# A list scheduler's positions, rounded to six decimals, in a fused attention and gated feed-forward kernel

## The chip, the cores and the metric

The kernel runs on one core of one Trainium2 chip. The metric is the device time of one execution in microseconds, the median of several runs. The profile is one more execution, taken by the hardware profiler; its durations are those of that execution.

## The reference, cut to what matters

Eight batches of eight heads, 1024 positions, head size 64. Keys and values are first projected along the sequence to 64 rows (E and F), then comes attention over those 64, and its output goes through a gated feed-forward layer.

```python
k_proj = einsum('ks,bhsd->bhkd', E, k)
v_proj = einsum('ks,bhsd->bhkd', F, v)
scores = (q @ k_proj.T) / sqrt(64)                  # per batch and head: 1024 x 64
attn = exp(scores - max) ; attn = attn / (sum + 1e-9)
x = attn @ v_proj                                   # -> 8192 tokens x 512
gate = 1 / (1 + exp(-(x @ w_gate)))                 # 512 -> 1536
out = (gate * (x @ w_val)) @ w_out                  # 1536 -> 512, float32
```

## The kernel before, in words

Each batch's 1024 tokens make two blocks of 512, so there are 16 blocks. The feed-forward layer is done block by block, mostly as Strassen-Winograd products with seven multiplications in place of eight: `quad_jobs(K)` makes a third of a block's hidden layer (three K to a block), with one call of `seven` for the gate (W = "G") and one for the value ("V"). The seven products are called A11, A12, S2, S1, S3, A22 and S4 after their left factor. They run on TensorE (PE) into PSUM banks; ScalarE (ACT) copies and snapshots the banks and takes the tanh; VectorE (DVE) adds partial results (`plus`, line 1156) and multiplies value by gate into `hT` (line 1225). `o_jobs(blk)` makes the output product of a block in the same way (sums of `hT` in `s_sum`, line 557, on VectorE or GpSimd (POOL); merges on VectorE, line 1414), or as a plain product (`o_plain`); SyncE (SP) issues the stores.

The attention of a batch is made while the feed-forward layer of the batch before is running. `kv_jobs` or `apart_jobs` project keys and values (`kpd`, `vpD`). `score_jobs` makes eight score tiles: `score` on PE (`kpD`, `qT`), then on VectorE the row maximum (`highest`, line 1645) and its subtraction in the bank (`lower`, line 1672), then the exponential on ScalarE into `pt` (which shares the memory `KVs`), and a DMA transpose to `eT`. `out_jobs` makes twelve out tiles: `outs` on PE (`vpD`, `eT`), reciprocals of the sums on VectorE (`invert`, line 1717), the division on VectorE or, after a copy by ScalarE, on GpSimd (`divide`, line 1734), and a DMA transpose to `xT`, from which the next batch's blocks read. All matmuls have line 528, all ScalarE operations line 542, GpSimd's loads line 569: they are issued by helpers.

None of this code fixes the order of the instructions. Each piece is a `Job` with an engine, a position `pos` on a common axis (one unit is about a sixth of a batch; the positions are sums of tuned offsets from the tables `AT` and `FB`) and the order of its creation, `rank`. `Scheduler.run` walks through a planned time: for each free engine it takes the first job, by position and then by rank, whose inputs are planned to be ready, whose PSUM bank or buffer is free, and whose position is not above that of the first matmul job not yet placed by more than `window` (43.429). The instructions are then issued in the order of the planned starts, and each engine runs its own in that order, waiting on semaphores. So one engine's order also decides which bank or buffer a job gets, when it comes free, and what can be taken next.

```python
for item in sorted(self.open[e], key=lambda i: (i[0], i[1])):   # position, then rank
    if item[0] > limit and not self.running(item[3]):
        continue
    if item[2] <= t + 1e-9 and self.take(item[3], t):
        best = item
        break
```

The positions are binary floating-point sums such as `pos + step * i + lag`, taken in different orders in different places.

Of the kernel before, what the change touches and what calls it, by code (L numbers as in the profile page):

```python
# [54 lines left out]
class Plan:  # L55
# [3 lines left out]
    def __init__(self):  # L59
        self.ops = []  # L60
        self.writers = {}
        self.readers = {}
        self.dma_count = {}
# [89 lines left out]

class Job:
    def __init__(self, eng, pos, body, release, name):
        self.eng, self.pos, self.body, self.release, self.name = eng, pos, body, release, name
        self.cost, self.bytes, self.dma, self.port = 0.0, 0, False, False
        self.deps, self.slots, self.start, self.end = {}, [], None, None

# [1755 lines left out]
```

## Time and profile before

| what | value |
|---|---|
| median of 3 runs | 528.46 us (528.36 to 530.05) |
| the profiled execution | 528.95 us |
| its span, first to last instruction | 527.2 us |
| mean granted TensorE clock | 0.997 |
| TensorE matmuls | 513.4 us busy, 4784 |
| VectorE | 448.3 us busy, 845 |
| ScalarE | 374.6 us busy, 716 and one table load |
| GpSimd | 166.0 us busy, 194 |

How to read it: busy times are sums over the span; matmuls overlap (one of 256 columns is listed with 273 ns, though the next starts earlier), so that their rate is read from start to start. In the views of waits, "A <- B: total, times, longest" says how long engine A stood still until B released it. In a timeline, "x12" are equal instructions that follow each other, and brackets hold the idle time ahead of the first and what ended it. The chain of waits is followed back from the last instruction. "xT", "hT", "KVs" and so on are the names of tiles; pF and pA are the two sets of four PSUM banks.

### The profile page before, as it was taken

The numbers are of one execution on the slowest core, as the hardware profiler recorded it, in microseconds if no ns is written. First come the engines' busy times: TensorE is split into PE (matmuls) and PEld (weight loads), VectorE is DVE, ScalarE is ACT, GpSimd is POOL, SyncE is SP. The second block draws the span as 40 slices with busy tenths as digits, with TensorE's granted clock in tenths as the row PEclk, the third lists the DMA queues.
The fourth block names the chain that finished last, engine by engine and source line by source line (L and its number), as shares of the span: only waits on it lengthen the run. The fifth ranks groups of instructions, "written<-read, shape, count | busy, mean of one in ns | idle before, by whom it ended". The sixth has DMA issues, their size and how long they took to land.

```text
span 527.2 us, 12327 instructions
## 1 busy us (share of the span) xinstructions
PE 513.4 (97%) x4784; PEld 427.8 (81%) x4784; DVE 448.3 (85%) x845; ACT 374.6 (71%) x717; POOL 166.0 (31%) x194
## 2 busy tenths in 40 slices
PE   5999999999979999999999999999999999999998
PEld 4655876888758888888898888888888888888885
DVE  5889997696898879997999879988799969998770
ACT  1565866688747789676976779766896679776852
POOL 9841006602156023540246003460235302530110
PEclk9999999999989999999999999999999999999999
DMA  9999917795478936899269973799177992711104
GB/s 164 197 199 207 194 35 163 165 203 99 71 170 134 202 86 102 171 188 194 49 116 174 185 149 62 181 161 234 33 116 164 182 195 49 141 54 41 41 2 160
DMA packets 140523, 71.59 MB, mean 136 GB/s; under 512 B 97200, under 2 KB 132272, under 8 KB 140464
## 3 DMA queue, kind: packets, MB, share of 16 engines
q0 software_dynamic: 35904, 29.89, 37.4%
q1 hardware_dynamic: 104560, 40.91, 36.7%
q8 instruction: 38, 0.62, 0.5%
q14 instruction: 21, 0.17, 0.1%
HBM read 60.29 MB, written 16.78 MB: 146 GB/s over the span
## 4 chain that ended last, share of the span: by engine, by line
PE 94%; DVE 4%; DMA 1%; ACT 0%; issue 0%; SPq 0%
PE pA L528 50%; PE pF L528 44%; DVE hT L1225 1%; DVE hS L557 1%; DMA EF<-in_F_dram 1%; DVE topf L1645 1%; DVE pA L1672 0%; DVE spare L1156 0%; DVE KVs L1734 0%; DVE ost L1414 0%; DVE pF L1672 0%; DVE inv L1717 0%; ACT ost L542 0%; DVE xS L557 0%; DVE pA L1156 0%
## 5 line engine op out<-in xcount | busy, mean ns | idle before, releaser
L557 POOL TENSOR_TENSOR hT<-hT,hS 128x512 bf16<-128x512 bf16 x42 | 50.3, 1219 | 224.9 <-PE pA L528 127.5
L542 ACT ACTIVATE spare<-pF 128x512 f32<-128x512 f32 (+2 forms) x164 | 91.5, 576 | 22.0 <-PE pF L528 14.9
L542 ACT ACTIVATE spare<-pA 128x512 f32<-128x512 f32 (+2 forms) x151 | 85.9, 581 | 25.7 <-PE pA L528 18.9
L542 ACT ACTIVATE spare<-spare 128x512 f32<-128x512 f32 x76 | 48.2, 634 | 17.3 <-DVE spare L1156 16.9
L528 PE MATMUL pA<-wO,hT 128*128 128x256 bf16 (+1 forms) x396 | 57.2, 289 | 0.2 <-ACT ost L542 0.2
L1734 POOL TENSOR_TENSOR KVs<-spare,inv 128x256 bf16<-128x256 f32 (+1 forms) x47 | 33.5, 720 | 64.2 <-ACT spare L542 39.3
L1156 DVE TENSOR_TENSOR spare<-pF,spare 128x512 f32<-128x512 f32 x60 | 40.8, 683 | 11.0 <-ACT spare L542 3.8
L1156 DVE TENSOR_TENSOR spare<-pA,spare 128x512 f32<-128x512 f32 x55 | 37.4, 682 | 11.9 <-ACT spare L542 4.5
L528 PEld LDWEIGHTS pA<-wO,hT 128*128 128x128 bf16 x396 | 38.1, 98 | 10.4 <-ACT ost L542 0.4
L1225 DVE SCALAR_TENSOR_TENSOR hT<-spare,pF 128x512 bf16<-128x512 f32 x59 | 39.7, 679 | 2.2 <-PE pF L528 0.6
L1225 DVE SCALAR_TENSOR_TENSOR hT<-spare,pA 128x512 bf16<-128x512 f32 x55 | 37.1, 680 | 4.9 <-PE pA L528 2.2
L528 PE MATMUL pF<-xT,wG 128*128 128x256 bf16 (+1 forms) x212 | 35.4, 289 | 0.0
L528 PE MATMUL pF<-xT,wV 128*128 128x256 bf16 (+1 forms) x208 | 34.6, 287 | 0.0
L528 PE MATMUL pF<-wO,hT 128*128 128x256 bf16 (+1 forms) x216 | 31.4, 291 | 0.9 <-DVE hT L1225 0.9
L528 PE MATMUL pA<-xT,wV 128*128 128x256 bf16 (+1 forms) x200 | 32.2, 284 | 0.0
L528 PE MATMUL pA<-xT,wG 128*128 128x256 bf16 (+1 forms) x196 | 31.3, 282 | 0.0
L528 PE MATMUL pF<-xS,wV 128*128 128x256 bf16 x200 | 29.9, 273 | 0.0
L528 PE MATMUL pA<-wT,hS 128*128 128x256 bf16 x216 | 29.2, 273 | 0.3 <-DVE hS L557 0.3
L528 PE MATMUL pF<-xS,tG 128*128 128x256 bf16 x192 | 28.8, 273 | 0.0
L528 PE MATMUL pA<-xS,tV 128*128 128x256 bf16 x184 | 27.6, 273 | 0.0
L528 PE MATMUL pF<-xS,wG 128*128 128x256 bf16 x184 | 27.3, 273 | 0.1
L528 PE MATMUL pA<-xS,wG 128*128 128x256 bf16 x176 | 26.3, 273 | 0.1
(177 smaller groups left out, 1295.6 us busy)
## 6 DMA issues: line engine op xcount, KB each, us to landing
out_dram<-ost SPq DMA_DIRECT2D x63, 256.0 KB, 2.4
KVs<-in_v_dram POOLq DMA_DIRECT2D x15, 512.0 KB, 9.4
KVs<-in_k_dram POOLq DMA_DIRECT2D x14, 512.0 KB, 6.9
Qb<-in_q_dram POOLq DMA_DIRECT2D x14, 512.0 KB, 12.8
wO<-in_moe_w_out_dram POOLq DMA_DIRECT2D x1, 1536.0 KB, 28.6
wG<-in_moe_w_gate_dram POOLq DMA_DIRECT2D x5, 256.0 KB, 16.6
wV<-in_moe_w_val_dram POOLq DMA_DIRECT2D x5, 256.0 KB, 17.2
KVs<-in_k_dram POOLq DMA_DIRECT2D x4, 256.0 KB, 6.6
```

What stands on the lines that cost most here:

```text
L528: lambda e: e.matmul(o, lhsT, rhs, **kw),
L542: lambda e: e.activation(o, i, func, scale=scale),
L557: fn = lambda e: e.tensor_tensor(o, a, b, op)
L1156: lambda e: e.tensor_tensor(PB(b)[:, :] if stay else BF(s), PB(b)[:, :], BF(s), ALU.add),
L1225: lambda e: e.scalar_tensor_tensor(o, y.rearrange("p (j c) -> p j c", j=2), 1.0, x.rearrange("p (j c) -> p j c", j=2), ALU.add, ALU.mult,),
L1645: lambda e: e.tensor_reduce((top if by_pe(b, t, y) else topf)[:, n : n + 8], PB(bk)[:, :].rearrange("p (n k) -> p n k", n=8), mybir.AxisLi ...
L1734: fn = lambda e: e.tensor_tensor(xto.rearrange("p (g h d) -> p h g d", g=2, h=H)[:, hh[0] : hh[1], :, :], o[:, :, 0:DH].rearrange("p (h g) ...
```

## The change

`Job` rounds its position to six decimals when it is made. Nothing else is touched.

```diff
 class Job:
     def __init__(self, eng, pos, body, release, name):
-        self.eng, self.pos, self.body, self.release, self.name = eng, pos, body, release, name
+        self.eng, self.pos, self.body, self.release, self.name = eng, round(pos, 6), body, release, name
         self.cost, self.bytes, self.dma, self.port = 0.0, 0, False, False
```

The offsets in the tables have three decimals, so many positions are equal as decimal numbers though their sums differ in the last bit: there are 212 groups of such positions on one engine. Before, the last bit decides which job of a group comes first; now they are equal and the order of creation decides. In 34 of the 212 groups this turns the order round: 25 on TensorE, 6 on VectorE, 3 on ScalarE. The first in time is a pair of value products of two neighbouring thirds of a block, `VA22` of K = 2 at 5.619 and `VS3` of K = 1 at 5.619000000000001; others come back in each batch, such as `GS2` and `GA12` at 16.969, 22.969 and 28.969. No operation, shape, engine or DMA is added or removed. Since `run` places each job with what is free at that moment, the order after a turned pair can differ from there on.

## The prediction

> **What bounds the kernel now.** I read the page first, then the busy times by stretch, then the waits and the chain of the one stretch that differs from its neighbours, then the order of the instructions in the two built programs.
>
> The page's first lines:
>
> ```profile
> span 527.2 us, 12327 instructions
> PE 513.4 (97%) x4784; PEld 427.8 (81%) x4784; DVE 448.3 (85%) x845; ACT 374.6 (71%) x717; POOL 166.0 (31%) x194
> ```
>
> TensorE is the bound as a whole. A reordering adds and removes no instruction, so it can only change the time in which TensorE stands still. Busy times by stretch of one batch, with the mean granted clock after POOL, show where that is:
>
> ```profile
> core 0: us, PE busy (x) PEld busy (x) DVE busy (x) ACT busy (x) POOL busy (x), PEclk, DMA share, GB/s
> 126.00:187.10 61.10, 56.90 (x519) 47.42 (x518) 53.01 (x95) 41.88 (x81) 19.82 (x22) 0.97 0.73 137
> 187.10:248.10 61.00, 61.00 (x587) 53.39 (x586) 54.74 (x102) 46.80 (x91) 19.83 (x22) 1.00 0.81 146
> ...
> ```
>
> The later batches are full: 61.00 of 61.00 us, 587 matmuls. The stretch from 126 to 187 is not: 56.90 of 61.10, 519 matmuls, and a clock of 0.97. What a better order can win lies there (and a little near 85 us); what a worse order can lose lies anywhere. TensorE's waits in that stretch:
>
> ```profile
> PE pF L528 <- ACT spare L542: 1.1, 3, 0.6
> PE pF L528 <- DVE hT L1225: 0.9, 1, 0.9
> PE pF L528 <- DVE inv L1717: 0.6, 1, 0.6
> PE pA L528 <- ACT ost L542: 0.6, 1, 0.6
> PE pA L528 <- ACT spare L542: 0.5, 1, 0.5
> ```
>
> Many short waits for different things mean that one engine behind them is full. The chain of waits of this stretch names it: from 133.91 to 154.02 nearly every piece is VectorE's.
>
> ```profile
> 133.91 0.70 DVE topf L1645
> ...
> 152.56 0.61 DVE pA L1156
> 153.17 0.10 DVE inv L1717
> 153.27 0.70 DVE hT L1225
> 153.97 0.04 issue
> 154.02 3.69 PE pF L528 x20
> ```
>
> And the windows of these two pieces:
>
> ```profile
> 133.71:154.02 20.31, 16.20 (x158) 12.70 (x155) 20.07 (x45) 12.53 (x25) 5.33 (x8) 0.98 0.65 128
> 154.02:157.00 2.98, 2.98 (x16) 2.16 (x17) 2.98 (x5) 0.55 (x1) 1.88 (x2) 0.54 0.98 188
> ```
>
> VectorE works 20.07 of 20.31 us; then TensorE runs 3 us at 0.54 of its clock. Why the work piles up there is in VectorE's timeline just before: it waits for score tiles of batch 2 that come one by one.
>
> ```profile
> 127.57 0.69 DVE L1645 TENSOR_REDUCE topf<-pA 128x8 f32<-128x512 f32 x1 [2.01 <-PE pA L528]
> ...
> 131.07 0.69 DVE L1645 TENSOR_REDUCE topf<-pA 128x8 f32<-128x512 f32 x1 [1.60 <-PE pA L528]
> ...
> 133.91 0.69 DVE L1645 TENSOR_REDUCE topf<-pA 128x8 f32<-128x512 f32 x1 [1.42 <-PE pA L528]
> ```
>
> That is 5.03 us of idle time on the engine that is then 20 us behind.
>
> **The change, step by step.** It removes and adds nothing: both programs have 4784 matmuls, 845 VectorE and 716 ScalarE operations and the same DMAs. It decides ties. The first matmul that moves is the 541st, at 64.29 us. Leaving bank and buffer names aside, 651 of 4784 matmuls stand elsewhere, 575 of them before the 1651st (192.50 us); from there on 76 of 3134 move, 20 of 535 VectorE operations and 12 of 481 on ScalarE. GpSimd's and SyncE's queues differ only up to their 84th and 45th instruction.
>
> Term A, the pile at 134 us. In the order of before, the eight score tiles of batch 2 begin at matmuls 1094, 1128, 1156, 1170, 1178, 1188, 1192, 1196 (counted from 0), and the first outs follow at 1212: five tiles bunched, 12 matmuls ahead of the work that follows them. In the changed order they begin at 1072, 1088, 1100, 1114, 1130, 1142, 1146, 1156, and the first outs come at 1200, 40 matmuls behind the last. Price of before: from matmul 1160 (133.71) to 1313 there are 102 of 256 columns, 20 of 128 and 32 of 130. TensorE's timeline gives 0.109 us for the first kind (12 from 143.74 to 145.05), 0.055 for the second (4 from 136.34 to 136.56), 0.06 for the third (3 from 147.67 to 147.85): 11.12 + 1.10 + 1.92 = 14.1 us. They took 20.31, so 6.2 us are lost. In the changed order VectorE has 51 operations from the first tile's maximum to the last hT that the O product of block 3 needs: 34 on 512 fp32 at 0.60 (start to start: 137.04, 137.64, 138.24), 12 reciprocals at 0.10, 4 divides at 0.46, one short sum at 0.34: 23.8 us. TensorE has 266 matmuls beside them: 206 × 0.109 + 28 × 0.055 + 32 × 0.06 = 25.9 us. VectorE has 2.1 us to spare where it was 6 short; in the tightest piece (24 operations, 12.8 us, beside 148 matmuls, 13.9) it has 1.1. Term A is -6.2; if the spare time is used up by queueing, -4.8.
>
> Term B, the slow clock. Matmuls 1314 to 1333 took 3.69 us (chain above) and are worth 20 × 0.109 = 2.18: 1.5 us. It came right after 4 us in which PE was busy for 1.98. Without the pile I take it as gone: -1.5, or 0 if it has another cause. [...]
>
> Term C, two gaps near 85 us.
>
> ```profile
> 83.25 2.77 PE L528 MATMUL pA<-wO,hT 128*128 128x512 bf16 x12 [0.22 <-ACT ost L542]
> ...
> 91.56 1.48 PE L528 MATMUL pF<-wT,hT 128*128 128x256 bf16 x12 [0.69 <-ACT spare L542]
> ```
>
> The first waits for its bank, which the plain O product just before used; in the changed order that product takes another bank: 0.22 gone. The second waits for the snapshot of the bank that it goes on in; 8 matmuls of 130 columns now stand between, 8 × 0.06 = 0.48 of cover: 0.2 stays. Term C is -0.7.
>
> Term D, what gets tighter. The second attention transpose (xT) of batch 1 is issued at 89.43, lands a median 3.3 us later (3.0 to 4.6 in the trace) and is used at 94.66: 1.9 us to spare. In the changed order 52 matmuls instead of 76 lie between its last outs and that use, 4.9 us instead of 7.5. The path there is a reciprocal (0.19), a copy (0.39), a divide on GpSimd (0.61), its queueing, and 3.3 of landing: 4.8 to 5.3 us. I take +0.3; bounds 0 and +1.6 (a landing of 4.6). A merge of an O bank just ahead has about 2 matmuls too little cover: +0.2. Small waits in the new order of 64 to 190 us: +0.2, from 0 to 1.
>
> Term E, the repeating batches: the same sequence but for the 76 swapped matmuls, whose TensorE waits in before are at most the 0.25 at 285.53. 0, within ±0.5.
>
> Sum: -6.2 - 1.5 - 0.7 + 0.3 + 0.2 + 0.2 = -7.7. The profiled execution took 528.95 us (span 527.2 and 1.75 around it): 521.3 by its measure. It lies 0.49 above the median of 528.46, so the forecast of a median is 520.8.
>
> **The rivals.** Part is given back: the xT transpose lands late (+1.3 over what I took), and VectorE loses time beside GpSimd. The timeline has one such case: a short hS sum of 0.41 us takes 2.87 at 282.86 while GpSimd runs two hT sums of 2.29 together. In the changed order three of GpSimd's hT sums stand in a row in the O product of block 1, beside VectorE's own; one collision costs 2.87 - 0.41 = 2.5. Time: 522.1 with the first, 524.6 with both. Against it: only one of the two lies where cover is thin. [...]
>
> The slow clock stays though the pile goes: 520.8 + 1.5 = 522.3. [...] Against it: it is the only slow stretch inside the trace, and it starts in the worst 4 us of TensorE.
>
> The pile only moves. VectorE's 448.3 us are the same, and if its 51 operations take 8% longer than the 23.8 us, they exceed TensorE's 25.9 and the jam forms a few us later: 527 to 530. Against it: VectorE's idle 5.03 us before the pile are now used.
>
> Slower: the swapped matmuls of the repeating part hold back a late score tile in each of the five later batches, as batch 2 had it. Price: 7.7 each, 5 × 7.7 = 38.5, so 520.8 + 38.5 = 559. It decides once the stall passes 1.5 us in a batch, which eats the gain. Against it: VectorE is busy 54.74 of 61.00 us there, and the score tiles and outs of the later batches stand at the same places in both orders.
>
> That the change does nothing is out: the two orders differ.
>
> **How the numbers follow.** Forecast as summed 0.69, part given back 0.14, slow clock stays 0.05, pile moves 0.05, slower 0.07. This kernel can be told from no change from about 0.3% on, 1.6 us: faster means under 526.9. The first three are faster, 0.88; a moved pile is the same, 0.05; the last is 0.07. The low end is 520.8 less the 0.7 of term D, if none of it comes true, the 0.5 of term E, and the 0.1 by which the fastest run of before lies under its median: 519.5. The high end takes in both give-backs (524.6) and the 0.5 of term E: 525.1. Left out are the last two rivals and the tails.
>
> **What would show it.** Right: the stretch of batch 2 full like its neighbours (over 580 matmuls in 61 us), no slow clock inside, VectorE off the chain, one gap of about 0.2 near 91 us, the later batches unchanged. Wrong: a DMA wait on xT near 93 us (term D), a clock under 1 with no pile (term B), VectorE on the chain around 130 us (term A), or PE below 61.0 in any later batch (term E).

## The result, and the profile after

The changed kernel takes 520.15 us (median of 4 runs, 519.96 to 520.69) beside 529.25 us for the kernel before on the same chip: a ratio of 0.983, 95% interval 0.9807 to 0.9853. (The 529.25 is the median of four runs; the 528.46 of the table above was that of the first three, with the same spread, 528.36 to 530.05.) The forecast was 520.8. The profiled execution of after took 519.99 us, span 518.2.

The page of after, span and busy times, and the engines' shares of the chain that ended last:

```profile
span 518.2 us, 12331 instructions
PE 509.5 (98%) x4784; PEld 427.8 (83%) x4784; DVE 446.7 (86%) x845; ACT 373.9 (72%) x717; POOL 164.5 (32%) x194
...
PE 98%; DMA 1%; ACT 0%; SPq 0%; issue 0%
```

The work is the same, and VectorE (4% of the chain before) has gone from the chain. The busy times by stretch, of after, in the columns of before:

```profile
126.00:187.10 61.10, 61.10 (x592) 53.73 (x590) 55.90 (x104) 46.58 (x90) 19.94 (x23) 1.00 0.73 143
187.10:248.10 61.00, 61.00 (x588) 53.54 (x586) 54.97 (x103) 46.78 (x91) 20.02 (x23) 1.00 0.75 143
```

The stretch of batch 2 had 56.90 us of TensorE, 519 matmuls and a clock of 0.97. It is now as full as its neighbour: 592 matmuls, clock 1.00. TensorE's waits in the whole of after:

```profile
PE pF L528 <- DMA EF<-in_F_dram: 5.7, 1, 5.7
PE pF L528 <- ACT EF L542: 0.2, 1, 0.2
```

Only the first load and the 0.22 us near 91 us that the prediction left standing remain.

Where the 9 us went is read from the start of the n-th matmul in both traces, after less before: +0.21 at the 60th (the first load), -0.67 at the 800th, -8.38 at the 1440th, -8.97 at the last. So terms C and D give -0.88, A and B -7.71, the later batches -0.59. Inside A and B, the 1314th to 1334th matmul took 3.52 us before and 2.22 after: the clock is 1.3 of it, the stall 6.4.

TensorE's timeline shows what the order did at that place. Before, from 147.67 us on (start, duration, tile, brackets: idle time ahead and what ended it):

```profile
147.67 0.34 PE L528 MATMUL pF<-vpD,eT 128*128 128x130 bf16 x3
...
148.28 0.34 PE L528 MATMUL pF<-vpD,eT 128*128 128x130 bf16 x3
149.17 0.29 PE L528 MATMUL pF<-vpD,eT 128*128 128x130 bf16 x2 [0.56 <-ACT spare L542]
150.10 0.34 PE L528 MATMUL pF<-vpD,eT 128*128 128x130 bf16 x3 [0.64 <-DVE inv L1717]
150.60 0.34 PE L528 MATMUL pF<-vpD,eT 128*128 128x130 bf16 x3 [0.16 <-ACT spare L542]
150.78 0.28 PE L528 MATMUL pA<-vpD,eT 128*128 128x130 bf16 x2
151.40 0.34 PE L528 MATMUL pF<-vpD,eT 128*128 128x130 bf16 x3 [0.34 <-ACT spare L542]
152.28 0.34 PE L528 MATMUL pA<-vpD,eT 128*128 128x130 bf16 x3 [0.55 <-ACT spare L542]
152.62 0.29 PE L528 MATMUL pF<-vpD,eT 128*128 128x130 bf16 x2
152.75 0.38 PE L528 MATMUL pF<-wO,hT 128*128 128x256 bf16 x2
154.02 2.32 PE L528 MATMUL pF<-wO,hT 128*128 128x256 bf16 x10 [0.89 <-DVE hT L1225]
```

These are out tiles (`outs`), from 148.28 on eight of them directly behind one another on three banks (pF2, pF3 and pA3). Each tile's matmuls are worth 0.12 to 0.17 us, and five of the eight tiles stand still until a bank has been through a reciprocal on VectorE and a copy or a division. The same tiles in after, to the start of the second gap between them:

```profile
136.28 0.34 PE L528 MATMUL pF<-vpD,eT 128*128 128x130 bf16 x3
136.45 0.45 PE L528 MATMUL pA<-vpD,eT 128*128 128x130 bf16 x5
136.84 0.83 PE L528 MATMUL pA<-wT,hT 128*128 128x256 bf16 x6
137.51 0.60 PE L528 MATMUL pA<-xS,wG 128*128 128x256 bf16 x4
137.95 0.34 PE L528 MATMUL pF<-vpD,eT 128*128 128x130 bf16 x3
138.12 0.46 PE L528 MATMUL pA<-vpD,eT 128*128 128x130 bf16 x5
138.42 0.60 PE L528 MATMUL pF<-xS,tV 128*128 128x256 bf16 x4
```

At most three stand in a row, and 6 to 16 matmuls of products come before the next ones. No bracket is left.

What did not change is how long a bank is held. One tile divided by VectorE, its reciprocal and its division, in before and then in after:

```profile
148.74 0.18 DVE L1717 RECIPROCAL inv<-pF 128x6 f32<-128x6 f32 x1
149.41 0.55 DVE L1734 TENSOR_TENSOR KVs<-pF,inv 128x384 bf16<-128x384 f32 x1
```

```profile
136.83 0.30 DVE L1717 RECIPROCAL inv<-pA 128x6 f32<-128x6 f32 x2
137.62 0.55 DVE L1734 TENSOR_TENSOR KVs<-pA,inv 128x384 bf16<-128x384 f32 x1
```

From the start of the tile's last matmul (148.40 and 136.57) to the end of the division, this turn took 1.56 us before and 1.60 after. Counted to the end of the last operation that reads the bank, the nine tiles of before from 147.67 on took 1.04 to 2.02 us, median 1.33, and the twelve of after 1.06 to 1.97, median 1.31. So no engine serves a bank faster in the new order: TensorE has other matmuls to run during the turn.

### The profile page after: what moved, and what is told of

The parts are those of the page before. It is cut to its first block, busy times and chain, and to the rows that moved or that the text cites. A ratio compares the mean times of both kernels' runs of the same rounds, so it can differ in the third digit from the quotient of the medians.

```text
span 518.2 us, 12331 instructions
## 1 busy us (share of the span) xinstructions
PE 509.5 (98%) x4784; PEld 427.8 (83%) x4784; DVE 446.7 (86%) x845; ACT 373.9 (72%) x717; POOL 164.5 (32%) x194
## 4 chain that ended last, share of the span: by engine, by line
PE 98%; DMA 1%; ACT 0%; SPq 0%; issue 0%
PE pF L528 50%; PE pA L528 48%; DMA EF<-in_F_dram 1%; ACT EF L542 0%; SPq L629 0%; ACT ost L542 0%
## 5 line engine op out<-in xcount | busy, mean ns | idle before, releaser
L542 ACT ACTIVATE spare<-pF 128x512 f32<-128x512 f32 (+2 forms) x179 | 101.0, 582 | 27.0 <-PE pF L528 18.1
L542 ACT ACTIVATE spare<-pA 128x512 f32<-128x512 f32 (+2 forms) x139 | 79.0, 577 | 24.5 <-PE pA L528 16.5
L1156 DVE TENSOR_TENSOR spare<-pA,spare 128x512 f32<-128x512 f32 x72 | 48.7, 681 | 13.5 <-PE pA L528 6.5
L1734 POOL TENSOR_TENSOR KVs<-spare,inv 128x384 bf16<-128x384 f32 (+1 forms) x50 | 36.3, 732 | 67.7 <-ACT spare L542 46.2
L528 PE MATMUL pA<-wO,hT 128*128 128x256 bf16 (+1 forms) x348 | 49.3, 287 | 0.0
L528 PE MATMUL pA<-xS,wG 128*128 128x256 bf16 x264 | 39.2, 273 | 0.0
L1156 DVE TENSOR_TENSOR spare<-pF,spare 128x512 f32<-128x512 f32 x41 | 28.0, 683 | 7.9 <-ACT spare L542 5.2
L528 PE MATMUL pF<-xS,tV 128*128 128x256 bf16 x224 | 33.6, 273 | 0.0
L528 PEld LDWEIGHTS pF<-wO,hT 128*128 128x128 bf16 x264 | 25.4, 98 | 6.4
L528 PEld LDWEIGHTS pA<-xS,wG 128*128 128x128 bf16 x264 | 25.2, 98 | 5.1 <-issue 2.3
```

The lines of the kernel that those rows point to most:

```text
L528: lambda e: e.matmul(o, lhsT, rhs, **kw),
L542: lambda e: e.activation(o, i, func, scale=scale),
L1156: lambda e: e.tensor_tensor(PB(b)[:, :] if stay else BF(s), PB(b)[:, :], BF(s), ALU.add),
L1734: fn = lambda e: e.tensor_tensor(xto.rearrange("p (g h d) -> p h g d", g=2, h=H)[:, hh[0] : hh[1], :, :], o[:, :, 0:DH].rearrange("p (h g) ...
```

## The experiments

**One pair or many?** Of the 34 turned groups the first (the pair VA22 and VS3 at 5.619) was turned alone in e1, and all but it in e2.

```diff
 # e1
+        pos = round(pos, 6) if 5.6185 < pos < 5.6195 else pos
 # e2
+        pos = pos if 5.6185 < pos < 5.6195 else round(pos, 6)
```

> Of the 34 turned groups only the first pair (VA22 and VS3 at 5.619) is turned; all other positions keep their last bits. Planned order: 150 TensorE jobs stand elsewhere than before, 22 elsewhere than in the changed kernel (late ones); GpSimd's and SyncE's orders equal those of the changed kernel. Theory (this pair sets the order of the bank grants up to batch 2, and so takes away the pile of VectorE work): 520 to 521.2 us, the stretch of batch 2 full at 61 us of TensorE, no slow clock in it; the late 22 jobs are worth at most the 0.6 us by which the later batches ran ahead. Rival (several turned pairs are needed): between 524 and 529 us, with part of the pile left.

> All positions are rounded but those of that pair. Planned order: 24 TensorE jobs stand elsewhere than before, 150 elsewhere than in the changed kernel. Theory: the pile and the slow clock stay, 528 to 529 us, less at most 0.6 us in the later batches. Rival (several pairs are needed, each gives a part): 522 to 527 us.

e1: 520.77 us, ratio 0.9824 (0.9808 to 0.984). e2: 530.49 us, 1.0005 (0.9996 to 1.0015), beside 529.83 for before. The stretch of batch 2 in e1, then in e2:

```profile
126.00:187.10 61.10, 61.10 (x593) 53.66 (x591) 55.88 (x105) 47.30 (x91) 20.06 (x22) 1.00 0.73 143
```

```profile
126.00:187.10 61.10, 56.89 (x519) 47.41 (x518) 53.02 (x95) 41.88 (x81) 19.92 (x22) 0.97 0.73 137
```

One last bit, at 5.6 on the axis, makes the whole difference; the other 33 groups change nothing that these runs can tell.

**Is it the volume of VectorE's work?** e3 keeps the order of before and leaves out most of VectorE's maximum and subtraction for the score tiles of batch 2.

```diff
+            few = 8 if b == 2 else 64
-                    PB(bk)[:, :].rearrange("p (n k) -> p n k", n=8),
+                    PB(bk)[:, :].rearrange("p (n k) -> p n k", n=8)[:, :, 0:few],
 # the subtraction in `lower` likewise
```

> The order of before, instruction by instruction; for the eight score tiles of batch 2 VectorE's maximum and subtraction go over 8 of 64 columns (that part of the computation is left out), some 0.5 us less each by the row of 0.60, about 8 us less work between 124 and 154 us. Theory (the stall is VectorE's volume of work in a piece that is too short for it): the 6.2 us of stall shrink to under 1, no slow clock follows, 521 to 522 us. Rival 1 (the order of TensorE and its banks stalls by itself): 526 to 529 us. Rival 2 (the slow clock has another cause than the pile): the stall goes and the 1.5 us stay, 522.5 to 523.5 us, with the half clock near 148 us.

529.76 us, ratio 0.9995 (0.9984 to 1.0005): nothing. VectorE did get its time back, as the windows show (before, then e3; VectorE is the third busy time):

```profile
126.00:141.00 15.00, 14.14 (x144) 12.14 (x143) 10.34 (x20) 13.21 (x26) 3.47 (x4) 1.00 0.22 42
141.00:154.02 13.02, 9.77 (x91) 7.52 (x89) 13.02 (x32) 7.00 (x14) 4.74 (x8) 0.97 0.80 160
```

```profile
126.00:141.00 15.00, 14.24 (x146) 12.36 (x143) 4.38 (x18) 12.67 (x26) 3.37 (x3) 1.00 0.27 53
141.00:154.50 13.50, 10.27 (x95) 8.10 (x94) 12.47 (x33) 7.55 (x16) 5.67 (x8) 0.99 0.76 157
```

From 126 to 141 us it has 6 us less to do, and waits 6 us longer for the next tile. From 141 us on it is nearly as busy as before, and the stall ends no earlier. So the theory that e3 names first fell: work taken off VectorE ahead of a point where it waits for other engines changed nothing behind that point.

**How much had VectorE to spare in the new order?** e4, e7 and e8 keep the changed order and take the maximum of batch 2's score tiles more often.

```diff
+            more = 1 if b == 2 else 0        # e7: 2; e8: 10 for the last tile alone
+            for i in range(more):
+                e.tensor_reduce(spill[:, c : c + 8], x, mybir.AxisListType.X, ALU.max)
```

For the half clock two readings stood against each other: how busy TensorE was over a stretch, or how long its longest single gap was.

> The changed order; each of the eight score tiles of batch 2 has its maximum taken twice by VectorE, 8 x 0.60 = 4.8 us more work. Theory (VectorE had 2.1 us to spare, 1.1 in the tightest piece): 2.7 to 3.7 us of stall, 522.9 to 523.9 us, and 1.5 more if the half clock comes back. Rival (VectorE's spare is larger than was reckoned, since it starts the tiles earlier): under 0.5 us, 520 to 520.6 us.

> The changed order, with two more maxima for each score tile of batch 2, 16 x 0.60 = 9.6 us. e4 cost 4.85 us for 4.8, so VectorE had nothing to spare: 9.6 to 9.9 us more than the changed kernel, 529.7 to 530.5 us. The clock: TensorE would be busy for about half of the time in the worst 4 us (it was 2.76 of 4 in e4, without a half clock, and 1.98 of 4 in the kernel before, with one). [...]

> The changed order, with ten more maxima for the last score tile of batch 2, 6.0 us in one piece. If VectorE's work is one for one: 525.5 to 526.5 us. TensorE can run on with what is ready, so the stall is one gap of 3 to 5 us or a few: a half clock of 3.4 us after it by either reading, up to 1.7 us more.

e4: 525.07 us, ratio to before 0.9908 (0.9893 to 0.9923). e7: 530.76 us (1.0013, 0.9999 to 1.0027). e8: 527.99 us (0.996, 0.9945 to 0.9975). Their traces against that of after, from the start of the same matmuls ahead of the place and behind it: e4 lost 4.7 us for 4.8 us of work. e7 lost 11.0 for 9.6, of which 1.6 is the half clock, and e8 7.8 for 6.0, of which 2.3 is. So it is nearly one for one. After's windows say why nothing was spare (in each 4 us TensorE and VectorE, the first and third busy time, are both full):

```profile
129.00:133.00 4.00, 4.00 (x46) 3.68 (x45) 4.00 (x7) 3.89 (x9) 0.00 (x0) 1.00 0.19 38
133.00:137.00 4.00, 4.00 (x42) 3.54 (x40) 4.00 (x10) 3.97 (x9) 0.00 (x0) 1.00 0.83 159
137.00:141.00 4.00, 4.00 (x46) 3.68 (x45) 4.00 (x13) 3.21 (x8) 2.87 (x4) 1.00 0.51 100
```

In e4 TensorE waits for the banks of the score tiles, which ScalarE's exponential frees once VectorE has been there:

```profile
PE pF L529 <- ACT KVs L543: 2.0, 3, 1.2
PE pA L529 <- ACT KVs L543: 0.4, 1, 0.4
PE pF L529 <- ACT pF L543: 0.2, 1, 0.2
```

e7 put the half clock back and e8 doubled it; their lines stand with the clock, below.

**VectorE's later work.** Its sums and hidden values between the last score tile and the end of the stall come next. e5 made the sums of the thirds 4 and 5 lighter.

```diff
+            few = 64 if K in (4, 5) else 512   # e5;  e9: K in (10, 11)
-                lambda e: e.tensor_tensor(PB(b)[:, :] if stay else BF(s), PB(b)[:, :], BF(s), ALU.add),
+                # the same on [:, 0:few] of each
 # e10: as e9, and the hidden values of K = 10, 11 on 32 of 256 columns of each half
```

> The order of before; the eight sums of VectorE at line 1156 of the thirds K = 4 and K = 5, which stand between the last score tiles and the end of the stall, go over 64 of 512 columns (part of the computation left out), about 0.45 us less each, 3.6 us together. e3 had shown that lighter score tiles change nothing: VectorE only waited longer for them, and from its 237th operation on it ran at the same times as before. Theory 2 (what TensorE waits for are the eight out tiles in a row, matmuls 1291 to 1313: each bank comes free after a reciprocal that is queued on VectorE behind sums and hidden values, so VectorE's work after the tiles counts): 2.5 to 5 us faster than before, 524 to 527 us. Rival (the loop outs, reciprocal, copy, next outs has its own latency on two or three banks, whatever else VectorE does): less than 1 us faster, 528.5 to 530 us.

The thirds 4 and 5 belong to block 1, some 60 us ahead of the stall. The sums of the stalled stretch kept their 0.68 us, and the time did not move: 529.8 us, 0.9996 (0.9986 to 1.0007). The run says only that lighter sums in block 1 are worth nothing.

> e5 again in the right place: the eight sums between the last score tiles and the end of the stall belong to the thirds K = 10 and K = 11 (block 3), not 4 and 5, whose sums run some 60 us earlier. The order of before; those sums go over 64 of 512 columns (left out in part), 8 x 0.45 = 3.6 us less VectorE work. Theory 2 (VectorE is late from 141 us on, because it waited for the score tiles until then; what it still owes the products of block 3 sets the pace of the outs and of the O product): 2.5 to 4.5 us faster than before, 525.2 to 527.3 us, and the half clock goes if the work of TensorE in no 3.4 us falls under about 0.4 of its rate. Rival (the loop outs, reciprocal, copy, next outs, on two or three banks): less than 1 us faster.

> As e9, and the hidden values (value by gate) of the same thirds go over 64 of 512 columns too, six of them in that piece, 6.3 us less VectorE work together. Theory 2: 5.5 to 7.7 us faster than before, no half clock, 522 to 524.4 us. Rival: less than 1 us faster; in between, the loop of the outs sets what stays of the stall.

e9: 528.43 us, 0.9966 (0.9955 to 0.9978). e10: 528.52 us, 0.9967 (0.9954 to 0.9979), beside 530.24. Both missed theory 2's numbers by far. By the traces the gain at the 1440th matmul, counted from the 60th on since the first load differs from one execution to the next, is 0.4 us in e9 and 1.0 in e10; what makes up the rest of the 1.8 and 1.7 us between the medians is not known. In e10 VectorE is no longer full, and the out tiles stall all the same (window from the first of these out tiles to the O product's last ten matmuls, before and e10):

```profile
147.67:154.02 6.35, 3.22 (x33) 1.89 (x30) 6.35 (x20) 3.68 (x8) 3.90 (x6) 0.95 0.59 156
```

```profile
147.96:152.94 4.98, 3.23 (x33) 1.90 (x30) 3.66 (x19) 2.82 (x7) 3.20 (x5) 1.00 0.47 153
```

**The loop of the banks.** In e6 the reciprocals of two tiles of three read a constant (that part of the division is left out), and those banks no longer wait for VectorE. In e11 all reciprocals and VectorE's divisions do, and no bank of an out tile waits for VectorE. e12 is e10 and e11 together.

```diff
-                lambda e: e.reciprocal(inv[:, n0 : n0 + 2 * k], o[:, :, DH]),
+                lambda e: e.reciprocal(inv[:, n0 : n0 + 2 * k], ones[:, 0 : 2 * k] if off else o[:, :, DH]),
-                b=bk,
+                b=None if off and sched.now is None else bk,   # the plan is as before
 # e11: in VectorE's divisions likewise
```

> The order of before; in batch 2 the reciprocals of the out tiles that GpSimd divides read a constant instead of the bank (the division by the sums is left out there), so that ScalarE's copy, which frees the bank, no longer waits for VectorE. The work on every engine is the same. Theory 2: about two thirds of the 4.3 us that matmuls 1284 to 1313 lost come back, 2 to 4 us, and the half clock after it may go too (1.3): 524 to 528 us. Rival (VectorE's volume alone: the O product's matmul 1314 waits for hT anyway, which comes at VectorE's pace): less than 0.7 us faster, 528.5 to 530 us; the stall then stands as one gap ahead of matmul 1314.

> The order of before. Batch 2's reciprocals, and VectorE's divisions, read a constant instead of the banks of the out tiles (that part of the computation is left out), so that a bank of an out tile is held by ScalarE's copy alone (two tiles of three) or by nothing; the work on each engine is the same. e6 and e10 each took away one of two limits and left the stall: e6 the reciprocal in the loop of the banks, e10 VectorE's volume. Theory 3 (both limits are about equally long, so that neither alone shows): with the loop cut alone VectorE's volume still sets the hT that matmul 1314 waits for: less than 1.2 us faster, 528.5 to 530.2 us, the stall moved from the outs to the O product. Rival (the loop alone is the cause): 3 to 6 us faster, 524 to 527 us.

> e10 and e11 together: no loop over VectorE, and 6.3 us less VectorE work after the score tiles. Theory 3: the 4.3 us between matmuls 1284 and 1314 and the half clock go, less what e10 lost later beside GpSimd (1.3 us): 4 to 6 us faster than before, 524 to 526 us. Rival 1 (VectorE's volume or the loop alone): no better than e10 or e11. Rival 2 (a third limit, such as ScalarE's copies or the landing of the transposes eT): less than 2.5 us faster.

e6: 530.13 us, 1.0004 (0.999 to 1.0017). e11: 530.57 us, 1.001 (1.0 to 1.0019). e12: 527.78 us, 0.9961 (0.9946 to 0.9976), beside 530.02. The stretch from the first of these out tiles to the O product's last ten matmuls, and those ten:

| order of before, with | stretch, us | last ten, us | ratio to before |
|---|---|---|---|
| nothing else | 6.35 | 2.32 | 1 |
| score tiles light (e3) | 6.35 | 2.31 | 0.9995 |
| reciprocals apart (e6) | 6.27 | 2.31 | 1.0004 |
| sums light (e9) | 5.97 | 2.31 | 0.9966 |
| sums and hidden values light (e10) | 4.98 | 1.26 | 0.9967 |
| loop cut at VectorE (e11) | 7.11 | 2.32 | 1.001 |
| e10 and e11 (e12) | 4.78 | 1.27 | 0.9961 |

The matmuls of the stretch are worth 2.03 us (24 × 0.0575 + 6 × 0.109). Theory 3 is right that cutting the loop alone gives nothing. It is wrong that both together free the stretch: 2.7 of the 4.3 us lost stay, and rival 2 of e12 held (2.2 us gained by the medians). The longest wait left in e12 comes from ScalarE's in-order queue:

```profile
149.90 0.63 ACT L543 ACTIVATE spare<-spare 128x512 f32<-128x512 f32 x1 [0.61 <-DVE spare L1157]
150.44 0.37 ACT L543 ACTIVATE spare<-pA 128x260 f32<-128x260 f32 x1
```

TensorE wants the bank pA of an out tile. Its copy stands behind a tanh, and that had waited 0.61 us for a sum on VectorE. TensorE then waits 1.09 us. e10 and e12 also pay about 1.1 us again near 159 us, in a wait for an `xS` sum that was not on the path before.

## Why the prediction was right, and where it was not

**Place and sum: right, the last digit in part by luck.** It named the stretch of batch 2 and forecast -7.7 for A and B; -7.71 was measured between the 800th and the 1440th matmul. Its price, what these matmuls are worth against what they took, needs no theory of who holds them up. The whole change was forecast as -7.7 and measured as -8.97 by the traces: terms C and D came to -0.88 where 0.0 was forecast, E to -0.59, and the first load was 0.21 later. The median missed by 0.65 us alone because the forecast also took off 0.49, by which the profiled execution lay above the median of three runs; after's profiled execution lies 0.16 below its median.

**Term A's reading of the cause: wrong.** The step "VectorE has 2.1 us to spare where it was 6 short" failed twice, and with it the inference that many short waits for different things mean one full engine behind them. VectorE was not short by its volume: 6 us less work in front of the stall gave nothing (e3), and 6 us less inside it 1.7 us (e10), with the half clock gone. Being busy 20.07 of 20.31 us was no proof that VectorE was the bound. Nor had it 2.1 us to spare afterwards: 4.8 us more cost 4.7 (e4). In after its first maximum starts 1.1 us behind the first tile's matmul (125.14 against 124.01), and its last hT is done 0.79 us ahead of its use (149.50 against 150.29); the 2.1 us were mostly these two ends (1.9 by the trace), and neither helps a score tile in the middle. What the runs show in its place: in the order of before, eight out tiles stand in a row, and each turn of a bank runs through the in-order queues of VectorE and ScalarE, between block 3's products (in that stretch VectorE is busy for 6.35 of 6.35 us, ScalarE for 3.68). No single link taken away frees it. The order does: the turns are as long as before, median 1.31 us for 1.33, and other matmuls fill them. This row and the wait for hT right behind it are 4.3 of the 6.2 us of term A. Most of the other 1.9 were lost around the first three out tiles, at 138.5 to 140.3 us, where the longest listed wait is 0.60 us for ScalarE's copy to `ost`; no run looked into that. Which link sets which turn stays open too, and pulling the out tiles apart by hand in the order of before was not tried.

**Term B: right**, 1.3 us for 1.5, and gone with the stall. What stood ahead of each half clock is in the last section.

**Term C: right**, 0.22 and 0.69 became 0 and 0.22.

**Term D: none of its 0.7 us came.** The term is about the second transpose xT of batch 1. The transposes in before (the second and third) and in after (the first three):

```profile
89.43 2.83 SPq L1751 DMA_TRANSPOSE xT<-KVs  x2
```

```profile
88.21 4.72 SPq L1751 DMA_TRANSPOSE xT<-KVs  x3
```

Of the three in after, the second is issued at 90.32 us, lands at 93.54 and is used at 94.00: it had 0.46 us to spare. From the last matmul of its out tiles (88.68) to the landing it took 4.9 us, at the low end of the 4.8 to 5.3 reckoned; and the cover was 5.3 us instead of 4.9, of which 0.22 is the wait that term C left standing. So the term was mis-sized and not of the wrong kind: 0.5 us more on that path would have shown as a wait. The other two small waits of the term did not come either.

**Term E: -0.59**, just over its bound of 0.5. The 0.25 at 285 us is missing, but such a wait for `hS` comes and goes from one execution to the next: with the changed order's later batches, e4 shows one of 0.24 at 282 us and e8 one of 0.31 at 285, after none; with before's, e3 shows 0.51 and 0.59. The other 0.34 us have no listed wait.

**Rivals.** None came: the slow clock went, no collision with GpSimd reached TensorE, the pile did not re-form, and the later batches are full. One sum in them is off: 8% on top of 23.8 us makes 25.7, still under the 25.9 of TensorE; it would have taken 9%.

## What to carry to other kernels

When an engine is full over a stall, make its work lighter before calling it the cause: VectorE was busy for all of this one, and was not what held it up alone (6 us less of its work gave nothing in e3 and 1.7 us in e10). Price a reordering by what the matmuls are worth against what they took, and look for tiles in a row that each wait for a bank to come round; put other matmuls between them. Where two engines are both full without a wait, as here after the change, a microsecond added to one can cost a microsecond: on VectorE it nearly did (4.7 us for 4.8 in e4; without the half clock 9.4 for 9.6 in e7 and 5.5 for 6.0 in e8).

## What the runs showed of the hardware

**What stood ahead of a half clock.** Every half clock inside these traces lasted 3.413 us (before, from 153.36 to 156.78) or twice that (e8, from 139.69 to 146.52). TensorE's windows of that length around it, in before (the second of them comes just ahead of the half clock):

```profile
146.54:149.95 3.41, 2.37 (x24) 1.84 (x22) 3.41 (x9) 1.41 (x3) 0.70 (x1) 1.00 0.62 210
149.95:153.36 3.41, 1.98 (x18) 1.06 (x18) 3.41 (x14) 2.28 (x6) 2.65 (x5) 1.00 0.72 164
153.36:156.78 3.42, 2.76 (x14) 1.97 (x15) 3.42 (x5) 0.71 (x2) 2.42 (x3) 0.50 0.92 178
```

In e7, two windows that were not followed by a half clock, and one that was:

```profile
131.92:135.33 3.41, 1.80 (x21) 1.23 (x18) 3.41 (x7) 1.35 (x3) 0.00 (x0) 1.00 0.00 0
135.33:138.74 3.41, 1.89 (x16) 1.12 (x14) 3.41 (x7) 1.20 (x3) 0.00 (x0) 1.00 0.77 147
142.16:145.57 3.41, 1.54 (x16) 0.92 (x13) 3.41 (x6) 1.58 (x4) 0.00 (x0) 1.00 0.36 69
145.57:148.98 3.41, 3.34 (x21) 2.60 (x21) 2.47 (x10) 2.12 (x6) 1.40 (x2) 0.50 0.42 82
```

The listed busy time misleads, since short matmuls are listed longer than their rate (in before one of 130 columns with 0.22 us, while the next starts 0.0575 later). Counted by the start-to-start times (0.109, 0.0575 and 0.056 us for 256, 130 and 128 columns, each matmul in the window in which it starts), the windows ahead of a half clock held 0.33 of a full window (before, e2, e6), 0.32 (e5), 0.28 (e3), 0.30 (e9), 0.29 (e7), 0.20 (e11) and 0 (e8); the two in e7 that passed held 0.39 and 0.45. In e8 one gap emptied a window, and the next, filled to 0.23 at half clock, was followed by another half clock:

```profile
141.54 0.48 PE L529 MATMUL pF<-vpD,eT 128*128 128x130 bf16 x3 [5.30 <-ACT KVs L543]
```

So of these windows, counted back from a half clock in steps of its length, those filled to 0.33 or less were followed by one, and those filled to 0.39 and 0.45 were not; the 0.4 in e9's expectation was an estimate. Of those ahead of a half clock only e8's first was empty. The length of a single gap did not decide: the longest was 0.89 us in before, with a half clock behind it, and in e7 one of 2.44 us brought none. The filling alone does not decide either. This stretch of e10 holds 18 matmuls of 130 columns, 0.30 by the same count, and the clock stayed at 1.00:

```profile
148.91:152.32 3.41, 1.84 (x18) 1.01 (x18) 2.58 (x15) 2.30 (x6) 2.58 (x4) 1.00 0.41 156
```

The half clock came in every run of before taken beside e9, e10 and e12, in 5 of 6 of e9, and in none of the 6 of e10 and the 4 of e12. That it matters where such a window begins is the author's guess; no run shows it.

**With a constant in place of a bank, VectorE's divisions took longer beside GpSimd's.** In e12 VectorE's divisions read `ones` in SBUF instead of the bank. Two of the four, started early in one of GpSimd's divisions, take 1.16 and 1.06 us; before, beside GpSimd's divisions too, each took 0.52 to 0.55 from the bank. In e11, the same:

```profile
149.48 1.18 DVE L1739 TENSOR_TENSOR KVs<-ones,inv 128x384 bf16<-128x384 f32 x1
```

GpSimd's division ran there from 149.41 to 150.24, and VectorE's ended 0.42 us behind it. Where VectorE's started first (e12, at 140.19 against 140.22), it took 0.54 us and GpSimd's 1.20 instead of 0.82. This may be part of why e11 was no faster. What holds the two up is not shown.
